# Linear attention feeding a SwiGLU block: loads of 128 partitions, quadrant matmuls for x, and attention steps one unit earlier

## The chip, the cores and the metric

The kernel runs on one NeuronCore of one Trainium2 chip. The metric is the device time of one execution in microseconds (us). Comparisons between two kernels use the median of several runs on the same chip. Engines are named as in the profile: PE (TensorE matmul), PEld (its weight loads), DVE (VectorE), ACT (ScalarE), POOL (GpSimd), SP (SyncE, which here only issues DMAs). A suffix q, as in SPq, means the queue of that engine where DMAs are issued.

## The reference: what is computed

Two stages follow each other. Sizes: batch B = 8, heads H = 8, sequence S = 576, head width D = 64, so 4608 tokens of width 512; the feed-forward width is 1536.

```python
q_s = softmax(q, axis=-1)            # over the 64 columns of a row
k_s = softmax(k, axis=2)             # over the 576 rows of a head
kv  = einsum('bhsd,bhse->bhde', k_s, v)
att = einsum('bhsd,bhde->bhse', q_s, kv)
x   = att.transpose(0, 2, 1, 3).reshape(4608, 512)
out = (silu(x @ w_gate) * (x @ w_val)) @ w_out
```

All inputs and the output are float32 in HBM. The kernel converts to bfloat16 on the chip and accumulates in float32.

## The kernel before, in words

**Attention.** Work is done per batch b and per group G of four heads (two groups per batch, 16 groups in all). `load` (L67) brings q, k and v of a group into float32 tiles of the pool `ld` (three buffers per tensor). A head's 576 rows lie on 64 partitions, nine rows on each, and the tile holds heads 4G and 4G+1 in its lower 64 partitions and 4G+2 and 4G+3 in its upper 64. Each half is a DMA of its own: 64 partitions, two heads, 2304 bytes in one piece.

`att_exp` (L114) takes the exponentials `eq` and `ek` on ACT and converts v into `vb`, whose column 128 is a constant one. `att_norm` (L128) sums `eq` over rows (`rs`), takes reciprocals (`rr`) and writes the normalized `qs`, all on DVE. `att_t` (L145) transposes `qs` on PE through the identity into two PSUM banks `tp` and copies them to `qt`. The name BANKS stands for the two pieces: five blocks of 64 tokens (320 columns) and four (256). `att_kv` (L162) does 18 accumulating matmuls of 64 rows, nine for each half g, so that `kv[g]` holds the 64x64 blocks of two heads on its diagonal and the sums of `ek` in column 128. `att_bd` (L176) scales these blocks by the reciprocal sums `kvr` into the block-diagonal tile `bd` (zero elsewhere). `att_x` (L186) multiplies: per half g one matmul with `bd` for 512 tokens (`xp`) and one for the last 64 (`x_tail`), 128x128 of TensorE each; ACT and DVE copy the results to `xt`, the transposed x of the whole problem.

**Feed-forward.** `m_unit(c0, n, m)` (L205), a *unit* below, computes 128 of the 1536 hidden columns for n tokens: four matmuls into `g_ps` and four into `u_ps` (one per 128 rows of x), then silu on ACT (`sg`) and the product on DVE (`hr`, a ring of 1536 tokens). A chunk of tokens takes 12 units, m = 0 to 11. `o_unit(j)` (L234) computes 128 tokens of the output from `hr`: 12 matmuls, a DVE copy to `o_sb`, two stores. The functions silu and exp need different tables on ACT, so each change between them is an ACT_TABLE_LOAD.

**Order.** The program runs under a manual schedule: every engine executes its instructions in the order in which the code emits them, and waits where an operand or a buffer isn't ready. All PSUM tiles come from one pool of eight banks.

- *Prologue.* The loads of batch 0 are issued on SP (the upper half of the first q on ACT). The first weight slice, issued on POOL, waits for the landing of v of group (0, 0). Then follow both groups of batch 0, up to `att_x(0, 1)`.
- *First chunk.* Twelve units over the 576 tokens of batch 0, each matmul in two pieces of 288 columns. The loads of batch 1 wait for the first slice of `wo`.
- *Batch 1* is done between the first four `o_unit`s.
- *Chunk loop.* Eight chunks, ci = 0 to 7: the first of 448 tokens (576 to 1023), the others of 512. In chunk ci, batch b = ci + 2 is done, as long as there is one (ci up to 5). `att_head(b, G)` is `att_exp` and `att_norm`; `att_steps` are three steps: `att_t`; `att_kv` with `att_bd`; `att_x`. Before, the heads are emitted ahead of units 4 and 8, together with two `o_unit`s each (not in ci = 0), and the steps behind units 5, 6, 7 and 9, 10, 11:

```python
if m % 4 > 0 and m > 4 and steps:
    steps.pop(0)()
```

So the last `att_x` of a batch comes directly before unit 0 of the next chunk, which reads it.

Of the kernel before, what the change touches and what calls it, by code (L numbers as in the profile page):

```python
# [15 lines left out]
def kernel(  # L16
# [8 lines left out]
    out: bass.AP,  # L25
):


# [32 lines left out]
    vbs = [const.tile([128, T, 130], BF16, name=f"vb{i}", tag=f"vb{i}") for i in range(2)]  # L61
    bds = [const.tile([128, 2, 128], BF16, name=f"bd{i}", tag=f"bd{i}") for i in range(2)]

    dmas = {}
    raw = {}

    def load(b, G, what, src, second=None, after=None):  # L67
        t_ = ld.tile([128, 2, T * 64], FP32, tag=what, name=what)
        for g in range(2):
            ap = bass.AP(  # L70
                tensor=src.tensor,
                offset=src[b, 4 * G + 2 * g].offset,
                ap=[[T * 64, 64], [HSTR, 2], [1, T * 64]],
            )
            eng = second if g == 1 and second is not None else nc.sync
            d = eng.dma_start(out=t_[64 * g:64 * g + 64], in_=ap)  # L76
            if after is not None and g == 0:
                tc.add_manual_dep(d.ins, after.ins.name, SYNC, reason="order of loads")
        dmas[what, b, G] = d
        raw[what, b, G] = t_  # L80

    def load_batch(b, after=None):
        for G in range(NG):
            for what, src in (("q", q), ("k", k), ("v", v)):
                load(b, G, what, src, nc.scalar if (b, G, what) == (0, 0, "q") else None, after)
                after = None
# [24 lines left out]
    st = {}  # L111
    BANKS = ((0, 5), (5, 9))

    def att_exp(b, G, v_eng):  # L114
        s = st[b, G] = {"bd": bds[G], "vb": vbs[G]}
        for what in ("q", "k"):
            e = at.tile([128, T, 2, 64], BF16, tag="e" + what, name="e" + what)
            nc.scalar.activation(  # L118
                out=e, in_=raw[what, b, G].rearrange("p h (t d) -> p t h d", d=64), func=AF.Exp
            )  # L120
# [54 lines left out]

    def att_bd(b, G):  # L176
        s = st[b, G]
        for g in range(2):
            kv = s["kv"][g]
            kvr = at.tile([128, 1], FP32, tag=f"kvr{g}", name="kvr")  # L180
            nc.vector.reciprocal(out=kvr, in_=kv[:, 128:129])
            for h in range(2):
                r = slice(64 * h, 64 * h + 64)
                nc.vector.tensor_scalar_mul(s["bd"][r, g, r], kv[r, r], kvr[r, :])

    def att_x(b, G):  # L186
        s = st.pop((b, G))
        qt = s["qt"].rearrange("p g t c -> p g (t c)")
        xp = [f_tile("xp") for _ in range(2)]
        tl = f_tile("x_tail").rearrange("p (g c) -> p g c", g=8)  # L190
        for g in range(2):
            nc.tensor.matmul(  # L192
                out=xp[g], lhsT=s["bd"][:, g, :], rhs=qt[:, g, 0:512], start=True, stop=True
            )
            nc.tensor.matmul(  # L195
                out=tl[:, g, :], lhsT=s["bd"][:, g, :], rhs=qt[:, g, 512:S],
                start=True, stop=True,
            )
        c0 = b * S
        nc.scalar.copy(out=xt[:, 2 * G, c0:c0 + 512], in_=xp[0])  # L200
        nc.vector.tensor_copy(out=xt[:, 2 * G + 1, c0:c0 + 512], in_=xp[1])  # L201
        nc.scalar.copy(out=xt[:, 2 * G:2 * G + 2, c0 + 512:c0 + S], in_=tl[:, 0:2, :])


    def m_unit(c0, n, m):  # L205
        ms = slice(m * 128, (m + 1) * 128)
        parts = [(c0, n)] if n <= 512 else [(c0, n // 2), (c0 + n // 2, n // 2)]
        gu = []
# [52 lines left out]
    with tc.manual_schedule():  # L261
# [4 lines left out]
        for vb in vbs:  # L266
            nc.vector.memset(vb[:, :, 128:129], 1.0)
        for bd in bds:
            nc.vector.memset(bd, 0.0)

# [15 lines left out]
        att_kv(0, 1)  # L286
        att_bd(0, 0)
        att_x(0, 0)
        att_bd(0, 1)
        att_x(0, 1)  # L290

# [9 lines left out]
        def att_steps(b, G):  # L301
            def kv_bd():
                att_kv(b, G)
                att_bd(b, G)
            return [lambda: att_t(b, G, nc.vector), kv_bd, lambda: att_x(b, G)]
# [17 lines left out]
        for ci, (c0, n) in enumerate(chunks):  # L323
# [55 lines left out]
```

## Time and profile before

| | |
|---|---|
| median of 3 runs | 352.37 us (352.28 to 354.62) |
| profiled execution, its own time | 350.33 us |
| span of that execution, first to last instruction | 348.6 us |
| PE busy | 317.0 us (91% of the span) |
| DVE / ACT / POOL busy | 188.5 / 152.6 / 27.2 us |
| moved by DMA | 42.81 MB, 123 GB/s over the span |

Rows of the timeline begin with the start and the length in us, then engine, line, operation, output<-inputs and a count; brackets at the end give the idle time of the engine just before and what ended it. Rows of the chain of waits begin in the same way. Rows of a table by windows give, for a stretch of the span, its length, the busy time and the number of instructions of PE, PEld, DVE, ACT and POOL, then the granted clock of TensorE, the mean busy share of the DMA engines and the GB/s that they wrote. The span begins at 0; the profiled execution's own time is 1.7 us longer than the span.

### The profile page before, as it was taken

The page shows a single profiled execution, that of the slowest core. Times are in us where ns is not written, and L with a number is a line of the kernel's source. Part 1 is how long each engine was busy: PE and PEld are TensorE (multiplying, and loading weights), DVE is VectorE, ACT ScalarE, POOL GpSimd, SP SyncE. Part 2 cuts the span into 40 slices and gives each one's busy share as a digit, 9 for nine tenths or more (in the row PEclk, how much of TensorE's full clock was granted, in tenths as well). Part 3 has the DMA queues.
Part 4 walks back from the last instruction along what each step waited for, and adds up shares of the span by engine and source line. Part 5 has one row for each costly group of instructions (what it writes and reads, how often), then busy time and mean ns, then how long its engine had stood idle before and what let it go on. Part 6 is the DMA issues. An engine that isn't in the chain of part 4 may idle for free.

```text
span 348.6 us, 5035 instructions
## 1 busy us (share of the span) xinstructions
PE 317.0 (91%) x1900; PEld 159.5 (46%) x1900; DVE 188.5 (54%) x354; ACT 152.6 (44%) x217; POOL 27.2 (8%) x31
## 2 busy tenths in 40 slices
PE   0269998998699999999999999999999999999994
PEld 0237773444344454444444444444445444444443
DVE  2553439647746674667466746674667433333331
ACT  3454353376655734563456345634663311322200
POOL 0620012111100011002100110011000000000000
PEclk9999999899999999999999999999999999999999
DMA  7999998999602990299029902990202021102123
GB/s 168 228 200 206 226 230 198 230 255 224 131 0 47 231 248 5 60 224 241 5 59 222 244 5 55 212 229 34 51 11 61 1 63 29 31 2 60 30 62 91
DMA packets 25577, 42.81 MB, mean 123 GB/s; under 512 B 2896, under 2 KB 8784, under 8 KB 25552
## 3 DMA queue, kind: packets, MB, share of 16 engines
q1 hardware_dynamic: 19440, 37.33, 46.6%
q0 software_dynamic: 5808, 4.72, 8.6%
q10 hardware_dynamic: 304, 0.43, 0.5%
q8 instruction: 15, 0.25, 0.3%
q14 instruction: 10, 0.08, 0.1%
HBM read 37.75 MB, written 9.44 MB: 135 GB/s over the span
## 4 chain that ended last, share of the span: by engine, by line
PE 80%; DVE 7%; DMA 7%; ACT 3%; issue 1%; SPq 1%; DVEq 0%; ACTq 0%
PE u_ps L213 25%; PE g_ps L213 25%; PE o_ps L238 24%; DMA v<-in_v_dram 5%; PE kv L168 2%; PE tp L152 2%; DMA k<-in_k_dram 2%; DVE xt L201 1%; DVE hr L222 1%; PE xp L192 1%; DVE qs L138 1%; DVE rs L132 1%; ACT L118 1%; ACT eq L118 1%; SPq L76 1%
## 5 line engine op out<-in xcount | busy, mean ns | idle before, releaser
L221 ACT ACTIVATE sg<-g_ps 128x512 bf16<-128x512 f32 (+2 forms) x120 | 65.0, 554 | 146.0 <-PE g_ps L213 145.9
L222 DVE TENSOR_TENSOR hr<-sg,u_ps 128x512 bf16<-128x512 bf16 (+2 forms) x120 | 74.8, 633 | 91.2 <-PE u_ps L213 89.5
L213 PE MATMUL g_ps<-xt,wg 128*128 128x512 bf16 (+2 forms) x480 | 114.1, 361 | 1.2 <-DVE xt L201 0.9
L213 PE MATMUL u_ps<-xt,wv 128*128 128x512 bf16 (+2 forms) x480 | 111.3, 359 | 0.0
L238 PE MATMUL o_ps<-wo,hr 128*128 128x512 bf16 x420 | 94.1, 380 | 0.0
L213 PEld LDWEIGHTS <-wv 128*128 128x128 bf16 x480 | 47.1, 98 | 49.0 <-issue 3.1
L213 PEld LDWEIGHTS <-wg 128*128 128x128 bf16 x480 | 45.2, 99 | 43.0 <-issue 2.0
L238 PEld LDWEIGHTS <-hr 128*128 128x128 bf16 x420 | 40.7, 98 | 49.0 <-issue 0.8
L132 DVE TENSOR_REDUCE rs<-eq 128x18 f32<-128x1152 bf16 x16 | 21.6, 1353 | 32.9 <-ACT eq L118 32.9
L243 DVE COPY o_sb<-o_ps 128x512 f32<-128x512 f32 x35 | 23.2, 685 | 22.1 <-PE o_ps L238 22.1
L152 PE MATMUL tp<-ident,qs 128*128 128x128 bf16 x144 | 12.2, 236 | 19.5 <-DVE qs L138 19.4
L138 DVE TENSOR_TENSOR qs<-eq,rr 128x1152 bf16<-128x1152 bf16 (+2 forms) x18 | 21.9, 1224 | 0.5
L108 POOL CAST vb_76<-v 128x1152 bf16<-128x1152 f32 x7 | 9.2, 1310 | 150.3 <-DMA v<-in_v_dram 89.1
L152 PEld LDWEIGHTS <-qs 128*128 128x128 bf16 x144 | 9.9, 105 | 24.0 <-DVE qs L138 21.2
L118 ACT ACTIVATE eq<-q 128x1152 bf16<-128x1152 f32 x16 | 18.6, 1163 | 4.8 <-DMA q<-in_q_dram 4.6
L118 ACT ACTIVATE ek<-k 128x1152 bf16<-128x1152 f32 x16 | 18.4, 1150 | 4.4 <-DMA k<-in_k_dram 4.4
L221 ACT ACT_TABLE_LOAD x14 | 18.0, 1283 | 0.2
L200 ACT CAST xt<-xp 128x512 bf16<-128x512 f32 x16 | 9.4, 586 | 17.6 <-PE xp L192 9.4
L118 ACT ACT_TABLE_LOAD x13 | 16.7, 1283 | 0.2
L168 PEld LDWEIGHTS <-ek 64*128 64x128 bf16 x288 | 9.7, 102 | 8.5 <-ACT sg L221 5.0
L201 DVE CAST xt<-xp 128x512 bf16<-128x512 f32 x16 | 10.9, 684 | 3.4 <-PE x_tail L195 3.4
L108 POOL CAST vb_77<-v 128x1152 bf16<-128x1152 f32 x7 | 9.0, 1289 | 44.9 <-DMA v<-in_v_dram 24.9
(38 smaller groups left out, 102.0 us busy)
## 6 DMA issues: line engine op xcount, KB each, us to landing
k<-in_k_dram SPq DMA_DIRECT2D x32, 288.0 KB, 8.8
v<-in_v_dram SPq DMA_DIRECT2D x32, 288.0 KB, 9.7
out_dram<-o_sb SPq DMA_DIRECT2D x70, 128.0 KB, 2.4
q<-in_q_dram SPq DMA_DIRECT2D x31, 288.0 KB, 7.7
wo<-in_moe_w_out_dram POOLq DMA_DIRECT2D x3, 512.0 KB, 18.7
wg<-in_moe_w_gate_dram POOLq DMA_DIRECT2D x2, 384.0 KB, 11.0
wv<-in_moe_w_val_dram POOLq DMA_DIRECT2D x2, 384.0 KB, 12.2
wg<-in_moe_w_gate_dram POOLq DMA_DIRECT2D x1, 512.0 KB, 16.8
```

Of the source, the lines that this page charges most:

```text
L108: eng.tensor_copy(out=out, in_=in_)
L118: nc.scalar.activation(out=e, in_=raw[what, b, G].rearrange("p h (t d) -> p t h d", d=64), func=AF.Exp)
L132: nc.vector.reduce_sum(out=rs, in_=eq2, axis=mybir.AxisListType.X)
L138: nc.vector.tensor_mul(qs[:, t0:t1, :].rearrange("p t (h d) -> p (t h) d", d=64), eq2[:, 2 * t0:2 * t1, :], rr[:, 2 * t0:2 * t1].to_broadc ...
L152: nc.tensor.transpose(out=tp[:, j * 128:(j + 1) * 128], in_=s["qs"][:, t, :], identity=ident)
L168: nc.tensor.matmul(out=kv[g][:, 0:129], lhsT=s["ek"][r, t, :, :].rearrange("p h d -> p (h d)"), rhs=s["vb"][r, t, 0:129], start=(t == 0), ...
L201: nc.vector.tensor_copy(out=xt[:, 2 * G + 1, c0:c0 + 512], in_=xp[1])
L213: nc.tensor.matmul(out=p_[:, 0:w_], lhsT=w[:, kk, ms], rhs=xt[:, kk, c:c + w_], start=(kk == 0), stop=(kk == KT - 1),)
L221: nc.scalar.activation(out=sg[:, 0:w_], in_=g_ps[:, 0:w_], func=AF.Silu)
L222: nc.vector.tensor_mul(hr[:, m, r:r + w_], sg[:, 0:w_], u_ps[:, 0:w_])
L238: nc.tensor.matmul(out=o_ps, lhsT=hr[:, m, r0:r0 + 128], rhs=wo[:, m, :], start=(m == 0), stop=(m == MT - 1),)
L243: nc.vector.tensor_copy(out=o_sb, in_=o_ps)
```

## The change

Five edits come together.

1. `load` issues one DMA of 128 partitions per tensor and group, always on SP. The partition stride runs through heads 4G and 4G+1, and the second dimension steps by two heads, so half g now holds heads 4G+g and 4G+g+2.
2. `att_bd` writes the scaled 64x64 blocks side by side into a small tile `kn` (two buffers) in place of the block-diagonal `bd`. In the prologue (split is true) the blocks of g = 1 are scaled on ACT.
3. `att_x` uses 64x64 quadrants of TensorE: per piece of BANKS four matmuls, rows of half h against columns of half g, into `xp[h]`; then one copy on ACT and one on DVE per piece. Eight matmuls of 320 and 256 columns stand in place of two of 512 and two of 64.
4. The first chunk's matmuls are cut into 320 and 256 columns, not 288 and 288, as the pieces of `att_x` are.
5. In the chunk loop the steps stand behind units 4, 5, 6 and 8, 9, 10, and the heads and `o_unit`s ahead of units 3 and 7; in chunk ci = 0 the heads stand ahead of units 1 and 5.

```diff
-    def load(b, G, what, src, second=None, after=None):
+    def load(b, G, what, src, after):
         t_ = ld.tile([128, 2, T * 64], FP32, tag=what, name=what)
-        for g in range(2):
-            ap = bass.AP(
-                tensor=src.tensor,
-                offset=src[b, 4 * G + 2 * g].offset,
-                ap=[[T * 64, 64], [HSTR, 2], [1, T * 64]],
-            )
-            eng = second if g == 1 and second is not None else nc.sync
-            d = eng.dma_start(out=t_[64 * g:64 * g + 64], in_=ap)
-            if after is not None and g == 0:
-                tc.add_manual_dep(d.ins, after.ins.name, SYNC, reason="order of loads")
+        ap = bass.AP(
+            tensor=src.tensor,
+            offset=src[b, 4 * G].offset,
+            ap=[[T * 64, 128], [2 * HSTR, 2], [1, T * 64]],
+        )
+        d = nc.sync.dma_start(out=t_, in_=ap)
...
-    def att_bd(b, G):
+    def att_bd(b, G, split):
         s = st[b, G]
+        kn = s["kn"] = at.tile([128, 2, 64], BF16, tag="kn", name="kn")
...
                 r = slice(64 * h, 64 * h + 64)
-                nc.vector.tensor_scalar_mul(s["bd"][r, g, r], kv[r, r], kvr[r, :])
+                if split and g == 1:
+                    nc.scalar.mul(kn[r, g, :], kv[r, r], kvr[r, :])
+                else:
+                    nc.vector.tensor_scalar_mul(kn[r, g, :], kv[r, r], kvr[r, :])
...
-        for g in range(2):
-            nc.tensor.matmul(
-                out=xp[g], lhsT=s["bd"][:, g, :], rhs=qt[:, g, 0:512], start=True, stop=True
-            )
-            nc.tensor.matmul(
-                out=tl[:, g, :], lhsT=s["bd"][:, g, :], rhs=qt[:, g, 512:S],
-                start=True, stop=True,
-            )
-        c0 = b * S
-        nc.scalar.copy(out=xt[:, 2 * G, c0:c0 + 512], in_=xp[0])
-        nc.vector.tensor_copy(out=xt[:, 2 * G + 1, c0:c0 + 512], in_=xp[1])
-        nc.scalar.copy(out=xt[:, 2 * G:2 * G + 2, c0 + 512:c0 + S], in_=tl[:, 0:2, :])
+        for t0, t1 in BANKS:
+            n = 64 * (t1 - t0)
+            xp = [f_tile("xp") for _ in range(2)]
+            for g in range(2):
+                for h in range(2):
+                    r = slice(64 * h, 64 * h + 64)
+                    nc.tensor.matmul(
+                        out=xp[h][64 * g:64 * g + 64, 0:n],
+                        lhsT=s["kn"][r, g, :],
+                        rhs=s["qt"][r, g, t0:t1, :].rearrange("p t c -> p (t c)"),
+                        start=True, stop=True,
+                    )
+            c0 = b * S + 64 * t0
+            nc.scalar.copy(out=xt[:, 2 * G, c0:c0 + n], in_=xp[0][:, 0:n])
+            nc.vector.tensor_copy(out=xt[:, 2 * G + 1, c0:c0 + n], in_=xp[1][:, 0:n])
...
-        parts = [(c0, n)] if n <= 512 else [(c0, n // 2), (c0 + n // 2, n // 2)]
+        parts = [(c0, n)] if n <= 512 else [(c0, 320), (c0 + 320, n - 320)]
...
-            steps = []
+            heads = {1: 0, 5: 1} if ci == 0 else {3: 0, 7: 1}
+            steps = {}
             for m in range(MT):
-                if m in (4, 8):
-                    if att:
-                        G = 0 if m == 4 else 1
-                        att_head(b, G)
-                        steps = att_steps(b, G)
-                        if G == 1 and b + 1 < B:
-                            load_batch(b + 1)
-                    if ci > 0:
-                        o_unit(first_o + (0 if m == 4 else 2))
-                        if not (final and m == 8):
-                            o_unit(first_o + (1 if m == 4 else 3))
+                if att and m in heads:
+                    G = heads[m]
+                    att_head(b, G)
+                    for i, f in enumerate(att_steps(b, G)):
+                        steps[4 + 4 * G + i] = f
+                    if G == 1 and b + 1 < B:
+                        load_batch(b + 1)
+                if ci > 0 and m in (3, 7):
+                    o_unit(first_o + (0 if m == 3 else 2))
+                    if not (final and m == 7):
+                        o_unit(first_o + (1 if m == 3 else 3))
                 m_unit(c0, n, m)
-                if m % 4 > 0 and m > 4 and steps:
-                    steps.pop(0)()
+                if m in steps:
+                    steps[m]()
```

Two places show what edit 5 does to an engine's order. The first is DVE in chunk ci = 0. Rows `rs`, `rr`, `qs` are the normalization of a head; `kvr` and `bd0` (or `kn`) belong to the step `att_bd` of group (2, 0); an `hr` row is the product of one unit. Before, from the `hr` of unit 6 on:

```order
L222 TENSOR_TENSOR hr_74<-sg_905,u_ps_900 128x448
L181 RECIPROCAL kvr_928<-kv_908 128x1
L184 TENSOR_SCALAR bd0_78<-kv_908,kvr_928 64x64 x2
L181 RECIPROCAL kvr_932<-kv_909 128x1
L184 TENSOR_SCALAR bd0_78<-kv_909,kvr_932 64x64 x2
L222 TENSOR_TENSOR hr_74<-sg_946,u_ps_941 128x448
L201 CAST xt_73<-xp_950 128x512
L132 TENSOR_REDUCE rs_964<-eq_959 128x18
L134 RECIPROCAL rr_966<-rs_964 128x18
L138 TENSOR_TENSOR qs_968<-eq_959,rr_966 128x1152
```

The same engine and place after, from the `hr` of unit 4 on:

```order
L225 TENSOR_TENSOR hr_74<-sg_871,u_ps_866 128x448
L107 COPY qt_874<-tp_875 128x2x320
L107 COPY qt_874<-tp_882 128x2x256
L131 TENSOR_REDUCE rs_893<-eq_888 128x18
L133 RECIPROCAL rr_895<-rs_893 128x18
L137 TENSOR_TENSOR qs_897<-eq_888,rr_895 128x1152
L225 TENSOR_TENSOR hr_74<-sg_921,u_ps_916 128x448
L181 RECIPROCAL kvr_945<-kv_924 128x1
L187 TENSOR_SCALAR kn_944<-kv_924,kvr_945 64x64 x2
L181 RECIPROCAL kvr_949<-kv_925 128x1
L187 TENSOR_SCALAR kn_944<-kv_925,kvr_949 64x64 x2
```

The normalization of group (2, 1) stood behind the scaling and the copy of group (2, 0); now it stands ahead of the scaling of group (2, 0).

The second place is ACT where chunk ci = 0 ends and chunk 1 begins. `sg` rows of 448 columns are units of ci = 0, those of 512 are of chunk 1; `xt` rows are the copies of `att_x(2, 1)`. Before:

```order
L221 ACT_TABLE_LOAD
L221 ACTIVATE sg<-g_ps 128x448 x4
L200 CAST xt<-xp 128x512
L202 CAST xt<-x_tail 128x2x64
L221 ACTIVATE sg<-g_ps 128x512 x4
```

And after:

```order
L224 ACTIVATE sg<-g_ps 128x448 x4
L204 CAST xt<-xp 128x320
L204 CAST xt<-xp 128x256
L224 ACTIVATE sg<-g_ps 128x448
L224 ACTIVATE sg<-g_ps 128x512 x3
```

The copies of the last x stood directly ahead of the first unit of the next chunk; now a unit of the old chunk lies between.

More of the change, by code (lines that the diff above doesn't have):

```diff
@@ L61 @@
     vbs = [const.tile([128, T, 130], BF16, name=f"vb{i}", tag=f"vb{i}") for i in range(2)]
-    bds = [const.tile([128, 2, 128], BF16, name=f"bd{i}", tag=f"bd{i}") for i in range(2)]
     dmas = {}
     raw = {}
-    def load(b, G, what, src, second=None, after=None):
+    def load(b, G, what, src, after):
         t_ = ld.tile([128, 2, T * 64], FP32, tag=what, name=what)
-        for g in range(2):
-            ap = bass.AP(
-                tensor=src.tensor,
-                offset=src[b, 4 * G + 2 * g].offset,
-                ap=[[T * 64, 64], [HSTR, 2], [1, T * 64]],
-            )
-            eng = second if g == 1 and second is not None else nc.sync
-            d = eng.dma_start(out=t_[64 * g:64 * g + 64], in_=ap)
-            if after is not None and g == 0:
-                tc.add_manual_dep(d.ins, after.ins.name, SYNC, reason="order of loads")
+        ap = bass.AP(
[4 more added lines that the diff above has]
+        d = nc.sync.dma_start(out=t_, in_=ap)
+        if after is not None:
+            tc.add_manual_dep(d.ins, after.ins.name, SYNC, reason="order of loads")
         dmas[what, b, G] = d
@@ L84, in load_batch @@
             for what, src in (("q", q), ("k", k), ("v", v)):
-                load(b, G, what, src, nc.scalar if (b, G, what) == (0, 0, "q") else None, after)
+                load(b, G, what, src, after)
                 after = None
@@ L114, in att_exp @@
     def att_exp(b, G, v_eng):
-        s = st[b, G] = {"bd": bds[G], "vb": vbs[G]}
+        s = st[b, G] = {"vb": vbs[G]}
         for what in ("q", "k"):
@@ L267 @@
             nc.vector.memset(vb[:, :, 128:129], 1.0)
-        for bd in bds:
-            nc.vector.memset(bd, 0.0)
         w_dma = []
@@ L286 @@
         att_kv(0, 1)
-        att_bd(0, 0)
+        att_bd(0, 0, True)
         att_x(0, 0)
-        att_bd(0, 1)
+        att_bd(0, 1, True)
         att_x(0, 1)
@@ L303, in kv_bd @@
                 att_kv(b, G)
-                att_bd(b, G)
+                att_bd(b, G, False)
             return [lambda: att_t(b, G, nc.vector), kv_bd, lambda: att_x(b, G)]
```

3 lines of the change are left out of this document (removed).

## The prediction

> **What bounds the kernel now.** First I read the page: the busy time of the engines, and PE's in 40 slices, in tenths.
>
> ```profile
> PE 317.0 (91%) x1900; PEld 159.5 (46%) x1900; DVE 188.5 (54%) x354; ACT 152.6 (44%) x217; POOL 27.2 (8%) x31
> PE   0269998998699999999999999999999999999994
> ```
>
> PE is nearly always busy from the fourth slice on. Time is to be had where it isn't: the first three slices (8.7 us each), the dip in the eleventh, and PE's own work. The chain in order of time shows the start:
>
> ```profile
> 2.42 6.35 DMA k<-in_k_dram
> 8.79 10.28 DMA v<-in_v_dram
> 19.15 1.16 ACT vb_77 L106
> 20.35 1.16 PE kv L168 x18
> 25.48 1.92 PE g_ps L213 x8
> ```
>
> Until 19.1 us everything waits for the loads of batch 0; about 6 us of attention follow, then the first unit. From there, the waits of PE (25.3 to 348 us; us in total, times, longest):
>
> ```profile
> PE tp L152 <- DVE qs L138: 5.5, 2, 3.1
> PE xp L192 <- DVE bd_78 L184: 2.0, 2, 1.6
> PE g_ps L213 <- DVE xt L201: 0.9, 5, 0.2
> ```
>
> The first row is the dip, two waits in chunk ci = 0. The second is batch 1, between the `o_unit`s; DVE's order there is unchanged, so it stays. The third is one short wait at the start of a chunk. So the change can work on four things: the prologue, chunk ci = 0, the chunk boundaries, and the PE time of x.
>
> **The loads.** By windows, the rate while only 64-partition loads run, and while only weights (128 partitions, converted on the way) run; then what the whole kernel read, the rate in 40 slices of the first 30 us, and the issue and landing of a weight slice:
>
> ```profile
> 8.70:18.30 9.60, 2.86 (x32) 2.23 (x32) 5.59 (x10) 4.64 (x4) 6.07 (x8) 1.00 1.06 225
> 18.50:37.50 19.00, 16.09 (x121) 11.23 (x121) 8.11 (x23) 8.82 (x19) 2.23 (x3) 1.00 1.30 204
> q0 software_dynamic: 5808, 4.72, 8.6%
> HBM read 37.75 MB, written 9.44 MB: 135 GB/s over the span
> GB/s 0 0 3 157 273 292 209 206 209 230 221 227 243 212 237 215 237 230 212 246 218 230 224 220 186 195 199 200 205 202 201 204 200 206 204 202 205 203 204 210
> 12.54 0.75 POOL L94 DMA_DIRECT2D wv<-in_moe_w_val_dram  x1
> wv<-in_moe_w_val_dram POOLq DMA_DIRECT2D x1, 256.0 KB, 8.6
> ```
>
> The loads write 225 GB/s. The weights write 204, but q, k and v are 3 x 9.44 = 28.3 MB of the 37.75 MB read, so 4.72 MB written were 9.44 MB read: the engines read 408 GB/s. For a 128-partition load in float32, where read and write are equal, the trace thus bounds the rate by 204 and 408 GB/s. I take 400, because then nothing in this trace has to be faster than it was; 225 means no gain. [...]
>
> Rows of the second group in the prologue:
>
> ```profile
> 14.04 1.16 ACT L118 ACTIVATE eq<-q 128x1152 bf16<-128x1152 f32 x1 [1.45 <-DMA q<-in_q_dram]
> 17.80 1.21 PE L152 MATMUL tp<-ident,qs 128*128 128x128 bf16 x9 [4.00 <-DVE qs L138]
> ```
>
> Data begin to move at about 2.4 us. Six tensors of 0.59 MB at 225 GB/s take 15.7 us, so they end at 18.1; `vb_77` starts at 19.15, so a landing shows 1.0 us later. At 400 GB/s a tensor takes 1.47 us: v of group 0 lands at 2.4 + 3 x 1.47 + 1.0 = 7.8, the second q at 9.3, the last v at 12.2. Then the loads no longer come last. From the second `eq` (14.04) to the end of its transposes (17.80 + 1.21) are 4.97 us of ACT, DVE and PE, so they end at 9.3 + 5.0 = 14.3, and `kv` starts at 14.35 in place of 20.35: **-6.0 us**. From `kv` to the first unit were 5 us; the scaling split between ACT and DVE and the doubled copies leave that as it is, within 0.3. The weights are the cover: the second slice was issued at 12.54 and landed 8.6 us later, at 21.1; everything on POOL follows the landing of v, 3.8 us earlier, so 17.3, and unit 0 starts near 19.3. Issue on SP costs nothing: one DMA stands where two stood. The 288 to 320/256 edit is free: the same 576 columns.
>
> **x on quadrants.** A steady chunk, PE rows around `kv` and x:
>
> ```profile
> 128.03 0.70 PE L168 MATMUL kv<-vb_77,ek 64*128 64x129 bf16 x18
> 128.66 1.04 PE L213 MATMUL g_ps<-xt,wg 128*128 128x512 bf16 x4
> 129.53 1.03 PE L213 MATMUL u_ps<-xt,wv 128*128 128x512 bf16 x4
> 130.40 0.38 PE L192 MATMUL xp<-qt,bd_79 128*128 128x512 bf16 x1
> 130.89 0.94 PE L213 MATMUL g_ps<-xt,wg 128*128 128x512 bf16 x3
> 132.22 1.02 PE L213 MATMUL u_ps<-xt,wv 128*128 128x512 bf16 x4
> ```
>
> Starts give the pace: four matmuls of 512 columns in 0.87 us, 0.42 ns per column. x takes 0.49 us. The 18 `kv` matmuls of 129 columns take 0.63 us where 0.98 would be due one after another, so the two row halves overlap, to 0.64 of the serial time. The trace has no matmul on column halves. Bounds for the new x, 4 x 576 columns: all four quadrants at once 0.24 us, none 0.97. I take the factor of `kv`, 0.62: +0.13 us for each of the 14 groups behind the prologue, **+1.8 us** (-3.5 to +6.7). [...]
>
> **The chunk boundary.** Above, `g_ps` and `u_ps` are 0.87 us apart in a unit, but 1.33 (130.89 to 132.22) where unit 0 follows x and needs its copies: 0.46 us lost. After the change unit 11, 1.73 us, covers the copies, which were through before 132.22, 1.33 us after x. Six boundaries: **-2.7 us**. Nothing else in a steady chunk moves relative to its neighbours: heads, `o_unit`s and steps all move by one unit together, and DVE's extra copy per group fits in its idle time.
>
> **Chunk ci = 0.** In time: the last load of batch 2 on SP, `sg` of unit 0 beside `g_ps` of unit 1, then the head of group (2, 0), its late transposes and its scaling, and the second group's transposes:
>
> ```profile
> 64.15 1.71 SPq L76 DMA_DIRECT2D v<-in_v_dram  x2
> 69.98 0.54 ACT L221 ACTIVATE sg<-g_ps 128x448 bf16<-128x448 f32 x1
> 69.98 0.92 PE L213 MATMUL g_ps<-xt,wg 128*128 128x448 bf16 x4
> 74.53 1.28 ACT L118 ACT_TABLE_LOAD   x1
> 78.70 1.36 DVE L138 TENSOR_TENSOR qs<-eq,rr 128x1152 bf16<-128x1152 bf16 x1
> 79.35 0.98 ACT L221 ACTIVATE sg<-g_ps 128x448 bf16<-128x448 f32 x2
> 79.98 1.15 DVE L222 TENSOR_TENSOR hr<-sg,u_ps 128x448 bf16<-128x448 bf16 x2
> 80.12 0.68 PE L152 MATMUL tp<-ident,qs 128*128 128x128 bf16 x9 [2.41 <-DVE qs L138]
> 82.97 0.17 DVE L181 RECIPROCAL kvr<-kv 128x1 f32<-128x1 f32 x1
> 83.99 0.58 DVE L184 TENSOR_SCALAR bd_78<-kv,kvr 64x64 bf16<-64x64 f32 x2
> 91.18 0.68 PE L152 MATMUL tp<-ident,qs 128*128 128x128 bf16 x9 [3.10 <-DVE qs L138]
> ```
>
> A head keeps ACT from silu for 4.82 us (74.53 to 79.35), and its `qs` ends 5.53 us after the table load (78.70 + 1.36); the scaling takes 1.60 (82.97 to 83.99 + 0.58). Before, PE waited 2.41 + 3.10 = 5.5 us for `qs`. With heads ahead of units 1 and 5, four units (1.51 us each, 7/8 of 1.73) lie before the transposes, and both waits go. But DVE now normalizes group (2, 1) before it scales group (2, 0), and PE's next step, x(2, 0), waits for that. Counted from the end of unit 0's `sg`: 4.82, then four `sg` of 0.49, is the second table load at 6.8; `qs` ends at 12.3; the `hr` of unit 5 (0.58) and the scaling end at 14.5. PE, half a us into unit 1 at the start, has done units 1 to 6, the transposes (0.68) and `kv` (0.63) at 9.9 and wants x there. New wait for the second half of the scaling: 14.5 - 9.9 = 4.6, of which x's first half covers 0.3: 4.3 us. **-1.2 us** against 5.5. Behind DVE's late scaling stand `hr` of unit 6 and the copies of x; units 7 and 8 find their banks free by then. The loads of batch 2 were all issued by 65.9 us, ahead of unit 1 at 69.98, and land faster now.
>
> A long wait has a second price. Three windows, with the granted clock third from the right:
>
> ```profile
> 58.80:62.20 3.40, 1.43 (x8) 0.33 (x6) 3.24 (x11) 0.59 (x1) 1.19 (x1) 0.97 1.00 251
> 62.20:65.70 3.50, 3.50 (x33) 2.36 (x32) 2.72 (x9) 0.27 (x1) 0.00 (x0) 0.54 1.02 228
> 89.50:93.00 3.50, 1.82 (x16) 1.20 (x17) 3.38 (x6) 2.23 (x4) 0.00 (x0) 1.00 0.80 171
> ```
>
> After a stretch with PE 42% busy the clock was 0.54 for 3.5 us, which loses 0.46 x 3.5 = 1.6 us; after 52% it stayed at 1.00. Waits of 2.4 and 3.1 us escaped; one of 4.3 hardly will: **+1.6 us**.
>
> **The sum** against the profiled execution's 350.33: -6.0 + 1.8 - 2.7 - 1.2 + 1.6 = -6.5, so 343.8 us. The runs' median, 352.37, stands 2.0 above that execution. If those 2 us are a window at half clock in one of the two waits that go, they don't carry over; if they are something constant, the result is 345.8. I take the middle, **345 us**.
>
> **The rivals.**
> *The loads are no faster.* What speaks for it: the weights, on 128 partitions, wrote only 204 GB/s, so about 220 may be what can be written at all. Then the prologue keeps its 25 us: 345 + 6 = 351 us. Chance 0.12.
> *The quadrants run one after another*, with their weight loads hidden: 0.97 us per group, +6.7 in place of +1.8: 350 us. Against it stands the overlap of `kv`'s halves. Chance 0.08.
> *Each quadrant matmul also waits for its own weight load*, which ends slower. A row of before has what such a load takes, from start to end:
>
> ```profile
> L168 PEld LDWEIGHTS <-ek 64*128 64x128 bf16 x288 | 9.7, 102 | 8.5 <-ACT sg L221 5.0
> ```
>
> Eight of 102 ns on top of 0.97 are 1.79 us, +1.30 in each of 14 groups: 345 + 18.2 - 1.8 = 361 us. It decides from x = 1.15 us on, where 14 x (1.15 - 0.62) = 7.4 eats the gain. `kv` at 35 ns per load and matmul speaks against it. Chance 0.06.
> *The weights push in between the loads of batch 0* once their slices are issued at 7.8, or the clock halves once more: 2 to 4 us back, 347 to 349. Chance 0.1. Before, the weights flowed only when the loads were through.
>
> **How the numbers follow.** The forecast, with 0.64, has its own range of about 341 to 348: loads between 306 GB/s, the middle of the bounds (1.93 us per tensor, -4.2 us), and 408, x between 0.4 and 0.75, one half-clock window more or fewer. About 1% (3.5 us) is what a measurement here tells from no change. Faster than 348.8: the forecast 0.64, most of the last rival 0.08, a little of the first two 0.04, so 0.76. Slower than 355.9: 0.06. The rest, 0.18, is within 1%. For 8 in 10 the range reaches up to 350.5, through the second and half of the first rival, and down to 341.
>
> **What would show it.** In the profile after: about 400 GB/s in the first 12 us, the first `g_ps` near 19 us; x near 0.6 us between neighbours in a steady chunk; no `g_ps` wait for `xt`; in chunk ci = 0 no wait of `tp` for `qs`, but one of about 4 us of `xp` for `kn`, with a low clock behind it. The prediction is wrong if the loads stay near 225 GB/s, if x takes over 1.1 us, or if `xp` waits in every chunk.

## The result and the profile after

| | before | after |
|---|---|---|
| median of 4 runs each, one chip | 353.5 us (352.28 to 354.86) | 343.62 us (342.29 to 344.97) |
| profiled execution, its own time | 350.33 us | 344.36 us |
| its span | 348.6 us | 342.2 us |

The ratio is 0.972, with a 95% interval of 0.9656 to 0.9784: the change makes the kernel faster, by 9.9 us between the medians and 6.0 us between the two profiled executions. The forecast was 345 us.

The page of the changed kernel: busy time, PE's 40 slices and the granted clock.

```profile
PE 318.6 (93%) x1934; PEld 158.7 (46%) x1964; DVE 189.1 (55%) x364; ACT 152.5 (45%) x221; POOL 25.1 (7%) x31
PE   0699998987999999999999999999999999999994
PEclk9999998996999999999999999999999999999999
```

The second and third slices, 2 and 6 before, are 6 and 9 now. The dip has moved from the eleventh slice to the tenth, and the granted clock has its lowest slice there too (a 6). The start of the chain in order of time (start, length, what):

```profile
2.23 7.29 DMA q<-in_q_dram
9.54 1.17 ACT eq L117
...
13.30 1.21 PE tp L151 x9
14.52 1.09 PE kv L167 x18
19.48 2.04 PE g_ps L216 x8
```

The chain no longer hangs on the last load (v of the second group) but on the second q, and from there on ACT, DVE and PE. By windows, the rate while the loads of batch 0 run:

```profile
3.00:11.00 8.00, 2.30 (x27) 1.69 (x27) 4.22 (x7) 4.64 (x4) 2.68 (x4) 1.00 1.03 390
```

390 GB/s, against 225 before. The waits of PE behind the start (17 to 345 us):

```profile
PE xp L197 <- DVE kn L187: 5.7, 4, 3.2
...
PE g_ps L216 <- ACT xt L204: 0.2, 1, 0.2
```

The waits of `tp` for `qs` are gone, and `xp` waits for `kn` instead: 3.18 of the 5.7 us in chunk ci = 0, 1.5 in batch 1, and 1.1 still in the prologue. Chunk ci = 0 in time, DVE and PE together:

```profile
76.67 1.36 DVE L137 TENSOR_TENSOR qs<-eq,rr 128x1152 bf16<-128x1152 bf16 x1
78.67 0.60 DVE L187 TENSOR_SCALAR kn<-kv,kvr 64x64 bf16<-64x64 f32 x2
79.01 1.84 PE L197 MATMUL xp<-qt,kn 64*64 64x320 bf16 x8 [3.18 <-DVE kn L187]
79.51 0.60 DVE L187 TENSOR_SCALAR kn<-kv,kvr 64x64 bf16<-64x64 f32 x2
80.78 1.68 PE L216 MATMUL g_ps<-xt,wg 128*128 128x448 bf16 x4
82.25 1.70 PE L216 MATMUL u_ps<-xt,wv 128*128 128x448 bf16 x4
```

DVE normalizes group (2, 1) (`qs`, to 78.03) before it scales group (2, 0) (`kn`). PE waits 3.18 us; then x itself is spread over 1.77 us (79.01 to 80.78), since its second half waits for the second scaling and the clock is at half meanwhile. Behind it four matmuls take 1.47 us between starts, about twice the usual 0.77. The clock, by windows of 3.41 us (the granted clock is the third number from the right; it changes at 57.93, 61.34, 78.41 and 85.23 us, 0.24 ahead of these cuts, hence the 0.96):

```profile
54.76:58.17 3.41, 2.21 (x23) 1.23 (x25) 3.21 (x11) 0.75 (x2) 0.00 (x0) 0.96 1.01 376
58.17:61.58 3.41, 3.19 (x24) 1.60 (x20) 2.35 (x9) 0.00 (x0) 1.15 (x1) 0.54 1.07 403
75.24:78.65 3.41, 0.59 (x4) 0.10 (x1) 3.33 (x5) 3.03 (x4) 0.27 (x1) 0.96 0.20 74
78.65:82.06 3.41, 3.01 (x12) 1.13 (x13) 2.66 (x8) 0.74 (x2) 0.00 (x0) 0.50 0.02 5
82.06:85.47 3.41, 3.41 (x12) 1.36 (x10) 0.62 (x1) 0.57 (x2) 0.00 (x0) 0.53 0.00 0
```

One window at half clock is in batch 1, as before the change; two more follow the wait in chunk ci = 0. A steady chunk around `kv` and x:

```profile
122.36 0.70 PE L167 MATMUL kv<-vb_77,ek 64*128 64x129 bf16 x18
...
123.86 1.03 PE L216 MATMUL u_ps<-xt,wv 128*128 128x512 bf16 x4
124.82 0.44 PE L197 MATMUL xp<-qt,kn 64*64 64x320 bf16 x8
125.19 1.04 PE L216 MATMUL g_ps<-xt,wg 128*128 128x512 bf16 x3
```

x starts 0.96 us after `u_ps`, and the next `g_ps` follows 0.37 us later. The whole span, cut at the starts of matmuls in both traces:

| stretch | before | after | difference |
|---|---|---|---|
| start to the first `g_ps` | 25.29 | 19.41 | -5.9 |
| to unit 0 of chunk ci = 0 (first chunk, batch 1) | 42.69 | 43.79 | +1.1 |
| chunk ci = 0 | 27.96 | 29.21 | +1.25 |
| the rest | 252.7 | 249.8 | -2.9 |
| span | 348.6 | 342.2 | -6.4 |

### The profile page after: what moved, and what is told of

Same layout as the page of the kernel before. It is cut to its first block, busy times and chain, and to the rows that moved or that the text cites. A ratio compares the mean times of both kernels' runs of the same rounds, so it can differ in the third digit from the quotient of the medians.

```text
span 342.2 us, 5050 instructions
## 1 busy us (share of the span) xinstructions
PE 318.6 (93%) x1934; PEld 158.7 (46%) x1964; DVE 189.1 (55%) x364; ACT 152.5 (45%) x221; POOL 25.1 (7%) x31
## 3 DMA queue, kind: packets, MB, share of 16 engines
q1 hardware_dynamic: 18816, 37.63, 34.4%
## 4 chain that ended last, share of the span: by engine, by line
PE 84%; DVE 5%; DMA 4%; ACT 4%; issue 1%; SPq 0%
PE g_ps L216 27%; PE u_ps L216 26%; PE o_ps L241 24%; PE kv L167 2%; PE xp L197 2%; DMA out_dram<-o_sb 2%; DMA q<-in_q_dram 2%; PE tp L151 2%; DVE rs L131 2%; ACT eq L117 1%; ACT L117 1%; DVE qs L137 1%; ACT sg L224 1%; PE o_ps L255 1%; DVE kn L187 1%
## 5 line engine op out<-in xcount | busy, mean ns | idle before, releaser
L216 PE MATMUL g_ps<-xt,wg 128*128 128x512 bf16 (+2 forms) x463 | 112.5, 365 | 1.0 <-ACT xt L204 0.2
L204 ACT CAST xt<-xp 128x320 bf16<-128x320 f32 (+1 forms) x32 | 11.3, 401 | 20.3 <-PE xp L197 20.3
L107 POOL CAST vb_76<-v 128x1152 bf16<-128x1152 f32 x7 | 8.0, 1149 | 140.7 <-DMA v<-in_v_dram 132.9
L187 DVE TENSOR_SCALAR kn<-kv,kvr 64x64 bf16<-64x64 f32 x60 | 17.0, 283 | 2.0
L197 PE MATMUL xp<-qt,kn 64*64 64x320 bf16 (+1 forms) x128 | 11.4, 324 | 5.8 <-DVE kn L187 5.7
L151 PEld LDWEIGHTS <-qs 128*128 128x128 bf16 x144 | 9.6, 102 | 15.2 <-DVE qs L137 12.2
L205 DVE CAST xt<-xp 128x320 bf16<-128x320 f32 (+1 forms) x32 | 13.0, 449 | 2.8 <-PE xp L197 2.8
```

Source lines behind the costliest of these rows:

```text
L151: nc.tensor.transpose(out=tp[:, j * 128:(j + 1) * 128], in_=s["qs"][:, t, :], identity=ident)
L187: nc.vector.tensor_scalar_mul(kn[r, g, :], kv[r, r], kvr[r, :])
L197: nc.tensor.matmul(out=xp[h][64 * g:64 * g + 64, 0:n], lhsT=s["kn"][r, g, :], rhs=s["qt"][r, g, t0:t1, :].rearrange("p t c -> p (t c)"), s ...
L205: nc.vector.tensor_copy(out=xt[:, 2 * G + 1, c0:c0 + n], in_=xp[1][:, 0:n])
L216: nc.tensor.matmul(out=p_[:, 0:w_], lhsT=w[:, kk, ms], rhs=xt[:, kk, c:c + w_], start=(kk == 0), stop=(kk == KT - 1),)
```

## The experiments

Theory: the loads on 128 partitions give some 6 us, the shifted steps some 3 us at the chunk boundaries, and chunk ci = 0 gives its waits of `qs` away for a wait of `kn` and a low clock. Rivals: the new layout of the heads or the smaller matmuls make the gain and not the loads; the quadrants cost PE time; the low clock and the runs' extra 2 us are constants.

### The loads in halves again

The changed kernel, each load as two DMAs of 64 partitions, heads placed as in the changed kernel.

```diff
-        d = nc.sync.dma_start(out=t_, in_=ap)
+        for g in range(2):
+            ap = bass.AP(tensor=src.tensor, offset=src[b, 4 * G + g].offset,
+                         ap=[[T * 64, 64], [2 * HSTR, 2], [1, T * 64]])
+            d = nc.sync.dma_start(out=t_[64 * g:64 * g + 64], in_=ap)
```

> The changed kernel with one thing undone: each load of q, k and v is again two DMAs of 64 partitions (the layout of the heads stays the new one). Theory (the width of the loads made the prologue shorter): the rate falls from 390 to about 225 GB/s, the first g_ps starts at about 25 us instead of 19.4, and the time rises by about 6 us, to 349 to 350. Rival (the new layout, the split scaling or one queue instead of two made the prologue shorter): the first g_ps stays below 21 us and the time within 2 us of 343.6.

Measured: 350.16 us (348.56 to 351.21, 10 runs), 0.9937 of before (0.991 to 0.9965). The rate and the first unit, from the windows and the timeline of this kernel:

```profile
8.70:18.30 9.60, 2.92 (x32) 2.23 (x32) 5.61 (x10) 4.62 (x4) 6.07 (x8) 1.00 1.06 221
25.59 2.10 PE L217 MATMUL g_ps<-xt,wg 128*128 128x320 bf16 x8
```

The loads are back at 221 GB/s and the first unit at 25.59 us, 6.2 later than with whole loads. The median, from another comparison, is 6.5 above the changed kernel's, and the span, 348.1 us, is 5.9 above its span. So most of the gain, two thirds by the medians and nine tenths of the 6.4 us between the spans of before and after, is the form of the loads, and neither the new layout nor the smaller matmuls. The two forms differ in the partitions of a DMA and in the number of DMAs, and no run parts these two. But the DMA engines have no gaps in either (share 1.06 here, 1.03 with whole loads), and between 3 and 11 us 907 packets were moved in the kernel before, with the same halves, and 1436 with whole loads, all but 97 and 84 of them of 2304 bytes. On the queue of the loads a packet took 151 ns on average (815 packets, 96.3% of 16 engines' 8 us) and 92 ns (1433, 102.9%). So each packet takes longer in halves; the loss isn't time between DMAs.

### The steps alone

The kernel before with the fifth edit only: its chunk loop is that of the changed kernel.

```diff
-                if m in (4, 8):
+                if att and m in heads:
...
-                if m % 4 > 0 and m > 4 and steps:
-                    steps.pop(0)()
+                if m in steps:
+                    steps[m]()
```

> The kernel before with the earlier steps of the chunk loop alone (edit 5); loads, x and pieces stay as before. Theory (the schedule gains 0.46 us at each of six boundaries, and in chunk ci = 0 it trades waits of 5.5 us for one of about 4 us and one or two windows at half clock): the steady chunk takes 34.5 us instead of 35.0, chunk ci = 0 is no shorter, the profiled span falls by 1 to 2.5 us; against the runs of the kernel before, which seem to hold 2 to 3 us of half clock that its profiled execution does not have, 0 to 4 us faster. Rival (the schedule alone is the gain): 8 to 10 us faster, with the first g_ps still at 25 us.

Measured: 348.66 us (346.76 to 349.29, 4 runs), 0.9859 of before (0.98 to 0.9919). In the steady chunks the x of group 0 comes every 34.54 us, against 35.01 before: 0.47 at each boundary, 2.8 in six. Chunk ci = 0 took 28.15 us here, before 27.96: its old waits went, and the first row of PE's waits and the windows show what came:

```profile
PE xp L192 <- DVE bd L184: 8.3, 6, 3.5
84.02:87.43 3.41, 1.45 (x8) 0.70 (x9) 3.25 (x10) 1.40 (x4) 1.15 (x1) 0.96 1.05 225
87.43:90.84 3.41, 3.41 (x12) 1.35 (x10) 0.79 (x2) 0.57 (x2) 0.00 (x0) 0.54 1.04 228
```

So the wait and the half clock in chunk ci = 0 come from the new order, not from the quadrants or the loads.

### The second head behind the first group's scaling

The changed kernel, with the second head of chunk ci = 0 ahead of unit 6: DVE then meets the scaling of group (2, 0) first.

```diff
-            heads = {1: 0, 5: 1} if ci == 0 else {3: 0, 7: 1}
+            heads = {1: 0, 6: 1} if ci == 0 else {3: 0, 7: 1}
```

> The changed kernel with the head of group (2, 1) in chunk ci = 0 moved ahead of unit 6 instead of unit 5, so that it stands behind the scaling of group (2, 0) on DVE and behind sg of unit 5 on ACT. Theory (the new wait of xp for kn, 3.2 us and half of x, and the two windows at half clock behind it come from that order alone): the wait goes, a wait of tp for qs of at most 1 us takes its place, the clock stays at 1.00 there, and the time falls by 5 to 8 us, to 336 to 339. Rival (PE waits there for banks or for ACT whatever the order): a wait of about the same length shows up elsewhere in chunk ci = 0 and the time stays within 2 us of 343.6.

Measured: 338.26 us (337.93 to 338.89, 4 runs), 0.9585 of before (0.9541 to 0.9628). PE's waits, x of group (2, 0) with the unit that follows it, and the one half-clock window that is left, with the window ahead of it:

```profile
PE xp L197 <- DVE kn L187: 2.5, 3, 1.3
PE g_ps L216 <- ACT sg L224: 0.5, 1, 0.5
75.36 0.96 PE L197 MATMUL xp<-qt,kn 64*64 64x320 bf16 x8
76.25 0.93 PE L216 MATMUL g_ps<-xt,wg 128*128 128x448 bf16 x4
54.11:57.52 3.41, 1.95 (x18) 1.03 (x17) 3.21 (x11) 0.75 (x2) 0.00 (x0) 0.96 1.02 366
57.52:60.93 3.41, 3.41 (x27) 1.75 (x26) 2.65 (x10) 0.00 (x0) 1.15 (x1) 0.54 1.06 403
```

x takes 0.89 us in place of 1.77 and starts without a wait, and `g_ps` keeps its usual pace of 0.77 us: the chunk takes 23.6 us (62.80 to 86.37) in place of 29.2. A new wait of 0.5 us for `sg` gives a little back. One number in a table was worth 5.4 us in the medians (4.8 by the two ratios to before, as the medians are of different comparisons): what DVE does first decided most of a wait of some 4.6 us on PE (3.18 and 1.77 - 0.37, the end of it at half clock) and the low clock behind it. The number also moves the second head behind `sg` of unit 5 on ACT, but the rows of the changed kernel show DVE as the cause: it held back `kn` until `qs` and one `hr` were done at 78.6, though the matmuls of `kv` had ended at 74.2. Of the 6.8 us at half clock PE stood waiting for some 1.6, so I estimate that they cost (6.8 - 1.6) / 2 = 2.6 us.

### The kernel before once more

> The kernel before, unchanged, to see its runs with span and clock one by one. Theory (the runs of before stand 2 to 4 us above its profiled execution because one or two more of its waits end in a window at half clock): runs with a lower mean clock are the longer ones, the clock goes down by about 0.005 for each 1.7 us, and the shortest run is about 350. Rival (a constant between profiled and timed executions): all runs have the clock of 0.995 and times of 352 to 355.

Measured: 351.57 us (350.01 to 355.16, 10 runs), ratio 1.0005 (0.9961 to 1.005). The prediction had carried half of the 2 us by which the runs of before stood above their profiled execution. The 36 runs of before that stand beside these experiments sort by the mean granted clock that each lists: 0.995 goes with 350.0 to 352.6 us (21 runs), 0.987 or 0.988 with 351.6 to 353.6 (10), 0.982 or 0.983 with 354.3 to 355.2 (5). In the profiles 0.995 belongs to the kernel before with one half-clock window, 0.989 to the steps alone with two, 0.984 to the changed kernel with three. So I take most of the 2 us to be half-clock windows that some executions have and others not. Inside one clock group up to 2.6 us are left, and the start explains part of it. The first units of this kernel, and those of the changed kernel:

```profile
25.70 2.11 PE L213 MATMUL g_ps<-xt,wg 128*128 128x288 bf16 x8
27.60 2.13 PE L213 MATMUL u_ps<-xt,wv 128*128 128x288 bf16 x8
29.52 1.37 PE L213 MATMUL g_ps<-xt,wg 128*128 128x288 bf16 x8
...
19.41 2.10 PE L216 MATMUL g_ps<-xt,wg 128*128 128x320 bf16 x8
21.30 2.13 PE L216 MATMUL u_ps<-xt,wv 128*128 128x320 bf16 x8
23.23 1.43 PE L216 MATMUL g_ps<-xt,wg 128*128 128x320 bf16 x8
```

Eight matmuls take 1.9 us between starts at first and 0.98 later, about the ratio of half to full clock (four of 448 columns took 1.47 us at 0.50 in chunk ci = 0, and 0.77 at 1.00). The windows list 1.00 for the slow ones too, because the trace's record of the granted clock begins only where the pace changes: at 27.9 us in the first profile of before, 30.0 here and 23.8 in the changed kernel, that is 2.6, 4.3 and 4.4 us after the first `g_ps`. The first chunks of the three took 24.77, 25.60 and 25.66 us, the first two with the same code. In the first profile of before the first chunk is half of that slow stretch and another 23.49 us, in the changed kernel half of it and 23.47. By this pace the changed kernel's 25.66 is thus the clock at the start and no cost of the change. From that first record on, the clock of the changed kernel was 1.00 for 34.13 us, 0.50 for 3.41, 1.00 for 17.07, 0.50 for 6.82 and 1.00 for 256.0: 10, 1, 5, 2 and 75 times 3.41 us; the last 0.9 us of the span, at 0.50, lie behind all matmuls. In the first profile of before it was 1.00 for 34.13 us, 0.50 for 3.41 and 1.00 to the end. What sets the length of the slow stretch at the start was not shown.

### x with the block-diagonal tile

The changed kernel with the second and third edits undone, but for the scaling split between ACT and DVE in the prologue. The loads stay, so heads 4G+1 and 4G+2 change places in the rows of x; the work is the same.

```diff
-                    nc.tensor.matmul(out=xp[h][64 * g:64 * g + 64, 0:n], lhsT=s["kn"][r, g, :],
-                        rhs=s["qt"][r, g, t0:t1, :].rearrange("p t c -> p (t c)"), ...)
+            nc.tensor.matmul(out=xp[g], lhsT=s["bd"][:, g, :], rhs=qt[:, g, 0:512], ...)
+            nc.tensor.matmul(out=tl[:, g, :], lhsT=s["bd"][:, g, :], rhs=qt[:, g, 512:S], ...)
```

> The changed kernel with x back on whole 128x128 matmuls with the block-diagonal tile (two of 512 columns, two of 64, three copies to xt), all else as changed. Because the loads put the heads differently, heads 4G+1 and 4G+2 change places in the rows of x, so the output is that of swapped heads; the work is the same. Reading A (from the changed kernel's trace: the eight quadrant matmuls stand 0.37 us apart from the next matmul, the four whole ones stood 0.49): x costs 0.49 us again, 0.03 to 0.12 us more per group, 14 groups: +0.4 to +1.7 us, so 343.6 to 345.5. Reading B (the prediction's term, +0.13 us per group for the quadrants): 1.8 us less than the changed kernel, 341.8.

Measured: 342.32 us (341.66 to 342.76, 4 runs), 0.9742 of before (0.9715 to 0.9769), whose interval overlaps that of the changed kernel. The same place of a steady chunk:

```profile
122.12 1.03 PE L216 MATMUL u_ps<-xt,wv 128*128 128x512 bf16 x4
122.98 0.38 PE L195 MATMUL xp<-qt,bd 128*128 128x512 bf16 x1
123.45 0.19 PE L198 MATMUL x_tail<-qt,bd 128*128 128x64 bf16 x1
123.47 1.03 PE L216 MATMUL g_ps<-xt,wg 128*128 128x512 bf16 x4
```

From `u_ps` to the next `g_ps` pass 1.35 us here and 1.33 with quadrants (123.86 to 125.19), where 0.87 would pass without x. The quadrants take 0.37 in place of 0.49 us, but start 0.96 and not 0.86 us after `u_ps`. What is left is 0.02 us per group, 0.3 us in 14 groups, far below what the times tell apart. So reading A holds for the steady chunks, just under its lowest figure. The median came out lower than A's range all the same, 1.3 us under the changed kernel's in another comparison, and nearer to B's 341.8, but not by B's cause. In the profiled execution it comes from ahead of the steady chunks: the first `g_ps` at 18.87 us and not 19.41, a first chunk of 25.1 and not 25.7 us, and 33.9 and not 34.4 us from unit 0 of chunk ci = 0 to the first `o_unit` of the chunk behind it, where, it seems, less of x stands behind the second scaling (two whole matmuls of four, not six quadrants of eight). The first two lie within the scatter of the start.

### Quadrants in another order

```diff
-        for t0, t1 in BANKS:
-            for g in range(2):
-                for h in range(2):
+        for g in range(2):
+            for h in range(2):
+                for xp, (t0, t1) in zip(xps, BANKS):
```

> The changed kernel with the eight quadrant matmuls in another order: both pieces (320 and 256 columns) of a quadrant one after the other, then the next quadrant, in place of all four quadrants for each piece. Same matmuls, same copies. Theory A (matmuls start in order, and overlap only where neighbours go to different quadrants): the second piece of a quadrant waits for the first, and the next quadrant starts with it, so x takes about 4 x 0.11 + 0.13 to 4 x 0.24 us, 0.5 to 0.9 in place of 0.37 us. Theory B (each quadrant has a queue of its own, so order doesn't matter): 0.37 us again, and the time stays within 0.5 us of the changed kernel's profiled 344.4. The prediction's factor 0.64 for overlap would be 0.62 us in both orders.

Measured, one execution: 343.99 us, x 0.38 us between its start and the next `g_ps`:

```profile
124.34 0.45 PE L196 MATMUL xp<-qt,kn 64*64 64x320 bf16 x8
124.72 0.39 PE L217 MATMUL g_ps<-xt,wg 128*128 128x512 bf16 x1
```

Theory B holds. The view of this one line shows why: first all that was in progress from 124.30 to 124.45, then from 124.45 to 124.60 (count, durations in ns, first and last start, forms):

```profile
L196 PE MATMUL xp<-qt,kn x4: 320/320/320, 124.3 to 124.4; 64*64 64x320 bf16 x4
L196 PE MATMUL xp<-qt,kn x8: 269/294/320, 124.3 to 124.5; 64*64 64x320 bf16 x4, 64*64 64x256 bf16 x4
```

The program orders 320, 256, 320, 256 and so on, yet by the records all four matmuls of 320 columns start first, and the four of 256 after them. The second matmul of a quadrant did not hold up the first of the next here.

### Batch 1: work from DVE to ACT, in two steps

The kernel with the second head ahead of unit 6, which still has a wait and a half-clock window in batch 1. First the copies `qt` and half the scaling of batch 1 go to ACT; then the first four copies `o_sb` as well.

```diff
-                att_bd(b, G, False)
-            return [lambda: att_t(b, G, nc.vector), kv_bd, lambda: att_x(b, G)]
+                att_bd(b, G, b == 1)
+            return [lambda: att_t(b, G, nc.scalar if b == 1 else nc.vector), kv_bd, lambda: att_x(b, G)]
```

> The changed kernel with the second head of chunk ci = 0 behind unit 5 (heads ahead of units 1 and 6), and in batch 1 the copies qt and the scaling of g = 1 on ACT, which is idle there. DVE's queue is then shorter by 0.7 + 0.6 us ahead of x(1, 0). Theory A (the half-clock window near 57 to 61 us follows from PE's wait of 1.3 + 0.2 us for kn just before it): the wait falls by about 0.6 us, and the window goes or stays with it: 336 to 338 against 338.3. Theory B (the window comes from the stage's whole busy share, whatever this one wait): window stays, 337.7.

```diff
-    def o_unit(j):
+    def o_unit(j, eng=nc.vector):
...
-        nc.vector.tensor_copy(out=o_sb, in_=o_ps)
+        copy(eng, o_sb, o_ps)
...
-        o_unit(0)
+        o_unit(0, nc.scalar)
```

> As the kernel before it in this list (copies qt and half the scaling of batch 1 on ACT), and the copies o_sb of the first four o_units on ACT too. DVE then has only the two normalizations and half the scaling, and x(1, 0) finds kn ready: DVE's second qs ends near 53.0 us, kn of g = 0 near 53.8, and PE wants x at 54.2. Theory A: no wait of xp for kn in batch 1 and no window at half clock behind it: 338.3 - 1.5 - 1.6 = 335.2 us. Theory B: the window has another cause and stays: 336.8 us.

Measured: the first step 337.41 us (335.85 to 337.8, 4 runs), 0.96 of before (0.957 to 0.9631); both 333.91 us (333.77 to 334.66, 4 runs), 0.9513 of before (0.949 to 0.9536). x(1, 0) in the first, x(1, 0) and the clock of the page in the second:

```profile
53.59 0.64 PE L197 MATMUL xp<-qt,kn 64*64 64x320 bf16 x2 [0.54 <-DVE kn L187]
54.45 0.76 PE L197 MATMUL xp<-qt,kn 64*64 64x320 bf16 x6 [0.22 <-ACT kn L185]
...
53.20 1.04 PE L197 MATMUL xp<-qt,kn 64*64 64x320 bf16 x8
PEclk9999999999999999999999999999999999999999
```

The wait went from 1.26 + 0.19 us to 0.54 + 0.22 and then to none in front of x (x itself still takes 0.97 us there, 53.20 to the next `tp` at 54.17), and the window at half clock went with it in both profiles. The first step's median lies near both theories; its profile, without a low window, speaks for A. The second settles it, 1.3 us below A's 335.2 and 2.9 below B's. Batch 1 with the four `o_unit`s took 18.1 us in the changed kernel and 14.65 in this one. Three of the first step's four runs were 1.5 to 2 us longer than its profiled one at a mean clock of 0.999 or 1.0; no trace of them exists, and why is open. The last kernel is the fastest here, 9.7 us below the change's median and 7.3 by the two ratios to before.

## Why the prediction was right, step by step

The time, the direction and the range held. The terms, against the two profiled executions:

| term | predicted | measured |
|---|---|---|
| prologue | -6.0 | -5.9 |
| x on quadrants | +1.8 (14 groups) | -0.2 (10 steady groups) |
| chunk boundaries | -2.7 | -2.7 |
| chunk ci = 0, waits and half clock | -1.2 + 1.6 | +1.25 |
| first chunk and batch 1 | 0 | +1.1 |
| outside the span | 0 | +0.4 |
| sum | -6.5 | -6.0 |

The rest of the run gained 2.9 us; ten groups of x at 0.02 are 0.2 of it, and the boundaries the other 2.7. The four groups of batch 1 and chunk ci = 0 are in the rows of their stages.

**The loads** were right in every step: 390 GB/s for the 400 assumed, the second `eq` at 9.54 for 9.3, `kv` at 14.45 in the timeline (14.52 in the chain) for 14.35, the first unit at 19.41 for 19.3. The bound worked: the loads came close below the 408 GB/s that the DMA engines had read during the weights in the trace of before. The rival that the loads are no faster fell with the 390 GB/s and with the first experiment. Of the rival with the weights and the clock, the weights held nothing up, since the last v was converted from 12.54 us on, against a landing forecast for 12.2; the clock did halve for one window more.

**x on quadrants is the mis-sized term**, by 2 us. The step that failed is the choice between 0.24 and 0.97 us: the prediction took the factor 0.64 of `kv`. All four quadrants run together, by the records of two orders, and 0.37 us with a start 0.10 later is still less than the 0.49 of the whole matmuls. What takes the 0.13 us above the bound of 0.24 was not tried. `kv`'s factor was the nearest row, but its matmuls are of 129 columns, 35 ns apart: a pace that need not hold for 320. The rivals by which quadrants run one after another, or wait for their weights, fell with it. The trace's 0.37 us stands nearer to the lower bound of 0.24 than to the 0.62 taken.

**The boundaries** were right: 0.47 us each in the kernel with the steps alone, and no `g_ps` waits for `xt` at a steady boundary. The row of five such waits in the prediction, 0.9 us in all, is one at the start of each of five chunks.

**Chunk ci = 0**: the mechanism was right, wait for wait. Predicted were 4.3 us of `xp` for `kn`; the trace has 3.18 in one piece and up to 1.4 more inside x, part of it half clock. The half clock came as foretold but lasted two windows and not one, some 2.6 us in place of 1.6: PE was still waiting in the first of them (81% busy from 78.41 to 81.82), and whether that gave the second was not shown. The other sizes make up the rest of the 0.85 us by which the stage missed. The third experiment shows that order alone did it.

**What wasn't foreseen** is +0.9 us in the first chunk, which by its pace is the clock at the start and which the kernel before shows too in its second profile, and 0.4 us outside the span (own time less span is 2.2 us here and 1.7 before). In the profiles of the experiments the second goes with the loads, 2.1 to 2.2 us in the five kernels with whole ones and 1.8 in the three with halves; its cause wasn't tried.

**The runs' extra 2 us** did not carry over, not even by half: the median of the changed kernel stands 0.7 us under its profiled execution, whose clock of 0.984 is that of the longer two of its four runs (0.988 and 0.989 in the others). That the forecast came so close is partly luck: 345 stood only 0.6 us above that execution because x, too dear by 2, and the 1.2 carried for the runs stood against some 2.5 that it lacked: 0.85 in chunk ci = 0, 1.1 in front of it, 0.4 outside the span and 0.1 in the prologue.

## What to carry to other kernels

Before a transfer is called bound by its rate, compare what the DMA engines read and wrote in another stage of the same trace: here the stage that converts on the way read 408 GB/s where the plain loads moved 225, and the form of a load, one DMA of 128 partitions (390 GB/s) or two of 64 (221), decided. When a step is moved earlier, read the order on the engine that feeds it, not only the step: one head placed ahead of a scaling on DVE cost PE some 4.6 us and the clock, by estimate, 2.6 more, and one number took most of it back. A wait that the clock's halving follows costs twice: in batch 1 waits of 1.26 + 0.19 us had a window of 3.41 us at a clock of 0.54 behind them, by estimate (0.46 x 3.41) another 1.6 us, and waits of 0.54 + 0.22 had none. So the 0.7 us between the two were worth more than their length.

## What the runs showed that was not expected

By the records the quadrants of TensorE were served like separate queues: with 320 and 256 columns alternating on each quadrant in the program, the records show the four of 320 starting together and the four of 256 after them, and x costs 0.38 us in place of 0.37. Theory A, by which matmuls start in order, gave 0.5 to 0.9 us; these records and the price of x speak against it.

PE's busy share in a window did not decide by itself here whether the clock halves. The windows are cut at the recorded changes of the clock and at multiples of 3.41 us from them. In the changed kernel a window with PE 58% busy (1.97 of 3.42 us, batch 1) was followed by a clock of 0.50. The kernel before kept the clock at 1.00 behind a window of chunk ci = 0 with 45% (second pair):

```profile
54.51:57.93 3.42, 1.97 (x19) 0.99 (x21) 3.22 (x12) 0.75 (x2) 0.00 (x0) 1.00 1.02 374
57.93:61.34 3.41, 3.19 (x24) 1.75 (x25) 2.59 (x10) 0.00 (x0) 1.15 (x1) 0.50 1.07 407
89.29:92.71 3.42, 1.53 (x15) 1.08 (x16) 3.35 (x7) 2.15 (x4) 0.00 (x0) 1.00 0.88 187
92.71:96.12 3.41, 3.41 (x35) 1.78 (x34) 2.62 (x9) 1.28 (x3) 1.15 (x1) 1.00 0.01 5
```

The 58% are x on quadrants, transposes and the start of `kv`; the 45% are transposes and six matmuls of units on the whole array. Whether that difference decides, or the modelled ends of the short matmuls in these shares, no run here tested; it stays open. The prediction's rule, 42% halves and 52% doesn't, held where it was used, but it is not the rule, and its 52% is the 45% above under other cuts.
